# First pair's hash as four 32x32 diagonal tiles on TensorE, with the opening steps in another order

## Chip, cores and metric

The kernel runs on one core of one Trainium2 chip. The metric is the device time of one execution in microseconds (us). Matrix work runs on TensorE (PE, with PEld for its weight loads), elementwise work on VectorE (DVE), ScalarE (ACT) and GpSimd (POOL); SyncE (SP) only issues DMAs. Each engine has its own instruction queue and works through it in order.

## What is computed

The program is a bucketed attention followed by a gated feed-forward stage. For each of 4 batches and 8 heads, 768 tokens of 64 values are hashed: a token's six hash bits are the signs of its products with `proj`, and a query sees only the keys with the same six bits.

```python
q_bits = (np.einsum('bhsd,dk->bhsk', q, proj) > 0)
k_bits = (np.einsum('bhsd,dk->bhsk', k, proj) > 0)
mask = q_bucket[:, :, :, None] == k_bucket[:, :, None, :]      # bucket = the six bits as a number
scores = where(mask, scale * q @ k.T, -1e9)
x = softmax(scores) @ v                                        # then (3072, 512), heads side by side
g = x @ w_gate
out = x + sigmoid(x @ w_res) * ((gelu(g) * (x @ w_val)) @ w_out)
```

The hash is done in float32, since a sign must not flip; the rest of the matrix work is bfloat16.

## The kernel before

**Units.** Two heads of one batch are a pair; there are 16 pairs, four to a batch. A pair's q (or k) is a tile of 128 partitions x 12 columns x 64 values: column c 0 to 5 is the first head, 6 to 11 the second. In what follows, Q0-4 are columns 0 to 3 of the first pair's q, K2-6 columns 2 to 5 of its k, and so on, as the slices in the code have it. A pair's scores are made in nine chunks of 128x1024 (`scores`, L500); the step `('S', n)` is chunk n, S0 to S8 are the first pair, S9 to S17 the second. The exponential of a chunk is one ACT instruction (L511), and `('V', n)` multiplies it with the values (L475). The score chunks share two PSUM buffers (`sc_ps`).

**How bits come about for the first pair.** `tr` transposes q or k in 32x32 blocks on DVE (L273), so that 32 of the 64 values lie on each group of 32 partitions. `hash_one` (L318) multiplies with `projs`, a 128x128 matrix that carries `proj` four times on its diagonal in blocks of 32; a column's two halves (`dh`) add up in PSUM. `bits_one` (L323, L325) transposes the sums back on DVE and writes the signs as six extra values behind each token in `nat`, which already holds the token cast to bfloat16 by `cast` (L261 on ACT, L263 and L265 on POOL). `turn_pe` (L373) transposes `nat` on TensorE into PSUM, and `turned` (the step `copy`, L379 on ACT, L381 on DVE) copies it into `aug`, the operand of the scores. The other pairs of the first batch use `hash_mm` (L284), which hashes two or four operands at once with weights of 32 columns, each in a column strip of its own (`tile_position=(0, 32 * j)`).

**Order.** All tiles and semaphores come from the framework, but the order on every engine is the order in which the steps are written out in `PLAN`; nothing is rescheduled. `PLAN` covers the first batch's attention (S0 to S35); then come that batch's gate and value products (L525), and from there a loop puts a batch's feed-forward matmuls between the next batch's score chunks. SP issues the loads of q, k and v in the order of `PLAN`; a load into a buffer that is used again waits for the last reader of the old data. Each of `ld0` (q) and `ld1` (k) has four buffers, so the fifth load of a kind, `('load', 5, side)`, takes the first pair's buffer, and `('load', 4, side)` the second pair's.

**The opening.** `fill` issues matmuls of 70 columns on constants (L229), 4 + 44 + 4 of them, ahead of the first hash on TensorE. PSUM tags that matter: `av` has two buffers, `r` and `f` one each; `w0` and `w1` are the two score buffers, borrowed for two of the hashes. The framework orders accesses to one PSUM bank, so a turn into a bank waits for the copy that still reads it.

Of the kernel before, what the change touches and what calls it, by code (L numbers as in the profile page):

```python
# [9 lines left out]
FP32 = mybir.dt.float32  # L10
# [5 lines left out]

PLAN = [
    ('load', 1, 0), ('load', 1, 1), ('load_v', 0), ('load', 2, 0), ('load_v', 1), ('load', 2, 1),
    ('load', 3, 0), ('proj', 's', 'pssp'), ('proj', 'w', 'pppp'), ('cast', 0, 1, 'p', 0, 6),
# [10 lines left out]
    ('vs', 0), ('load', 4, 0), ('load', 5, 1), ('load', 4, 1), ('load_v', 3),  # L30
    ('S', 0),
    ('S', 1), ('hash1', 0, 1, 6, 12, 'av'), ('bits1', 0, 1, 6, 12), ('turn', 0, 0, 6, 12, 'av'),
    ('copy', 0, 0, 6, 12, 'v'),
    ('S', 2),
    ('S', 3), ('hash', (1,), 2), ('turn', 0, 1, 6, 12, 'f'), ('hash', (1,), 3), ('hash', (1,), 0),
# [57 lines left out]
def kernel(  # L93
# [12 lines left out]
    nc = tc.nc  # L106
    B, H, S, D = q.shape
    NBITS = proj.shape[1]
    DMODEL = H * D
    DFF = moe_w_gate.shape[1]  # L110
    P = 128
# [24 lines left out]
    const = ctx.enter_context(tc.tile_pool(name="const", bufs=1))  # L136
# [55 lines left out]
    nc.vector.memset(eps_sb, EPS)  # L192
    table = const.tile([P, 1], BF16, name="table")
    nc.scalar.activation(table, warm[:, 0:1], AF.Exp)
    projs = const.tile([P, 2, P], FP32, name="projs")
    nc.gpsimd.memset(projs, 0.0)
    projr = const.tile([P, NBITS, D], FP32, name="projr")
    projw = const.tile([P, 2, 32], FP32, name="projw")
    nc.gpsimd.memset(projw, 0.0)
# [16 lines left out]
    def spread(dst, engs):  # L216
        for a, eng in enumerate(engs):
            if eng is nc.scalar:
                nc.scalar.activation(dst(a), projn, AF.Copy)
            else:  # L220
                eng.tensor_copy(dst(a), projn)
# [30 lines left out]
    def nat_of(x):  # L252
        return nat[(2 * x[0] + x[1]) % NN]

    def cast(p, side, eng, c0=0, c1=HT):
        x = (p, side)
        scale = (1.0 / C) if side == 0 else 1.0
        sl = slice(c0, c1)
        dst = nat_of(x)[:, sl, 0:D]
        if eng is nc.scalar:  # L260
            nc.scalar.activation(dst, raw[x][:, sl], AF.Copy, scale=scale)  # L261
        elif side == 0:
            eng.tensor_scalar(dst, raw[x][:, sl], scale, 1.0, op0=ALU.mult, op1=ALU.mult)  # L263
        else:
            eng.tensor_copy(dst, raw[x][:, sl])  # L265

    t32, hsum, htok = {}, {}, {}
# [8 lines left out]
    def hash_mm(jobs, dhs=(0, 1), hs_=(0, 1)):  # L276
        if jobs[0] not in hsum:
            hsum[jobs[0]] = mm_ps.tile([P, HT, 32], FP32, tag="r", name="hs")
        hs = hsum[jobs[0]]
        for hh in hs_:  # L280
            sl = slice(hh * T, hh * T + T)
            for dh in dhs:
                for j, x in enumerate(jobs):
                    nc.tensor.matmul(hs[32 * j:32 * j + 32, sl], projw[:, dh, :],  # L284
                                     t32[x][:, sl, dh, :], start=(dh == 0), stop=(dh == 1),
                                     tile_position=(0, 32 * j))
# [24 lines left out]
    def hash_one(p, side, c0, c1, tag):  # L311
        n, x = c1 - c0, (p, side, c0)
        if tag in ("w0", "w1"):
            hsum[x] = (wpt, wps)[int(tag[1])][:, 0:2 * n * 32].rearrange("p (i c n) -> p i c n", i=2, c=n)
        else:
            hsum[x] = (av_ps if tag == "av" else mm_ps).tile([P, 2, n, 32], FP32, tag=tag, name="hs1")
        for dh in range(2):
            nc.tensor.matmul(hsum[x][:, 0], projs[:, dh, :], t32[p, side][:, c0:c1, dh, :],  # L318
                             start=(dh == 0), stop=(dh == 1))

    def bits_one(p, side, c0, c1):
        hs = hsum[p, side, c0]
# [37 lines left out]
        nc.sync.dma_start_transpose(out=ag, in_=nat_of(x).rearrange("p c n -> p (c n)"))  # L360
        aug[x] = ag

    pts = {}

    def turn_pe(p, side, c0, c1, tag, pool=mm_ps):
        x = (p, side)
        if x not in aug:
            aug[x] = aug_pool.tile([P, HT, P], BF16, tag=f"aug{side}", name=f"aug{side}")
        k = (p, side, c0 // T)
        if k not in pts:  # L370
            pts[k] = pool.tile([P, T, P], BF16, tag=tag, name="pt")
        for c in range(c0, c1):
            nc.tensor.transpose(pts[k][0:KA, c % T, :], nat_of(x)[:, c, 0:KA], ident)  # L373

    def turned(p, side, c0, c1, eng):
        dst = aug[p, side][0:KA, c0:c1, :]
        pt = pts[p, side, c0 // T][0:KA, c0 % T:c0 % T + c1 - c0]
        if eng is nc.scalar:
            nc.scalar.activation(dst, pt, AF.Copy)  # L379
        else:  # L380
            eng.tensor_copy(dst, pt)  # L381
# [27 lines left out]
    av = {}  # L409
# [46 lines left out]
    def x_turn(b, hp):  # L456
        pt = mm_ps.tile([P, T, P], BF16, tag="f" if b == 0 else "r", name="pt")
        for t in range(T):
            nc.tensor.transpose(pt[:, t, :], x_tok[b][:, hp, t, :], ident)  # L459
        if hp == HP - 1:  # L460
            nc.scalar.activation(x_sb[b][:, hp, 0:2], pt[:, 0:2], AF.Copy)
            nc.vector.tensor_copy(x_sb[b][:, hp, 2:T], pt[:, 2:T])
        else:
            nc.vector.tensor_copy(x_sb[b][:, hp], pt)
# [238 lines left out]
    def first_gv(i):  # L703
# [2 lines left out]
    STEP = dict(  # L706
        S=score, V=value, fill=fill, tr=tr,
        proj=lambda w, engs: spread(
            (lambda a: projs[32 * a:32 * a + 32, :, 32 * a:32 * a + NBITS]) if w == "s" else
            (lambda a: projw[32 * a:32 * a + 32, :, NBITS * a:NBITS * (a + 1)]),  # L710
            [ENG[e] for e in engs]),
        cast=lambda p, side, e, *c: cast(p, side, ENG[e], *c),
        hash1=hash_one,
        bits1=bits_one,
        turn=lambda p, side, c0, c1, tag: turn_pe(p, side, c0, c1, tag, POOLS[tag]),
        copy=lambda p, side, c0, c1, e: turned(p, side, c0, c1, ENG[e]),
        turn_dma=turn,
        hash=lambda ps, i: hash_mm([(p, side) for p in ps for side in range(2)], (i % 2,), (i // 2,)),
        tokens=tokens, bits=lambda p, side, e: bits(p, side, [ENG[x] for x in e]),
        va=vals_a, vs=vals_s, finish=finish, open=opened, preset=preset, repeat=repeat,  # L720
        w=load_w, load=load, load_v=load_v, xturn=lambda hp: x_turn(0, hp),
# [10 lines left out]
    for s in range(NSLOT, LAST):  # L732
        p, c = divmod(s, NCH)
# [60 lines left out]
```

## Time and profile before

| what | value |
|---|---|
| time, three runs | 338.42, 338.57, 338.58 us; median 338.57 us |
| profiled execution: span from the first to the last instruction | 337.2 us |
| profiled execution: own time apart from the span | none is given on its page |
| PE busy | 332.7 us (99%), 3086 matmuls |
| DVE, ACT, POOL busy | 216.4, 213.8, 175.0 us |
| mean DMA rate over the span | 130 GB/s |

The span is what the engines' instructions cover; the timed runs hold 1.4 us more than it. Times inside the trace are counted from the span's start. PE's busy share is no measure of slack, since matmuls are pipelined and a fill counts as busy; the chain of waits, which goes back from the last instruction to what released it, shows which engine sets the time in which stage.

### The profile page before, as it was taken

How to read it: one execution, taken by the hardware profiler on the slowest of the kernel's cores; microseconds unless marked ns; L12 is line 12 of the kernel's file. 1: busy time of each engine (PE TensorE's matmuls, PEld its weight loads, DVE VectorE, ACT ScalarE, POOL GpSimd, SP SyncE). 2: the span in 40 equal slices, each digit the busy share in tenths (PEclk: the TensorE clock that was granted, in tenths of full speed). 3: DMA queues.
4: the chain of work that ended last, by engine and by line, in shares of the span. 5: the costliest groups of instructions: out<-in, count | busy, mean ns of one | idle time of the engine just before them, and what ended most of it. 6: DMA issues, size and time to landing. Idle time of an engine off the chain costs nothing.

```text
span 337.2 us, 7740 instructions
## 1 busy us (share of the span) xinstructions
PE 332.7 (99%) x3086; PEld 205.2 (61%) x3086; DVE 216.4 (64%) x458; ACT 213.8 (63%) x247; POOL 175.0 (52%) x260
## 2 busy tenths in 40 slices
PE   8999999999999999999999999999999999999996
PEld 8677666565666655665666665666566665666444
DVE  7977675664577958875687896876567444343243
ACT  4889962237999962437999982255999984322220
POOL 4779930234489942575999982567978100000000
PEclk9999999999999999999999999999999999999999
DMA  7998999999966233516149933923140340000012
GB/s 218 372 297 127 207 246 196 188 150 194 319 225 169 61 97 80 106 37 126 63 110 275 268 109 91 137 47 65 32 126 33 80 101 33 31 2 0 31 64 94
DMA packets 74387, 43.88 MB, mean 130 GB/s; under 512 B 52544, under 2 KB 71360, under 8 KB 74352
## 3 DMA queue, kind: packets, MB, share of 16 engines
q1 hardware_dynamic: 67872, 37.95, 45.6%
q0 software_dynamic: 6400, 5.44, 10.4%
q8 instruction: 24, 0.39, 0.5%
q14 instruction: 11, 0.09, 0.1%
q10 hardware_dynamic: 80, 0.00, 0.0%
HBM read 29.56 MB, written 6.29 MB: 106 GB/s over the span
## 4 chain that ended last, share of the span: by engine, by line
PE 93%; ACT 3%; DVE 1%; POOL 1%; issue 1%; DVEq 0%; ACTq 0%
PE sp L525 37%; PE fps L571 18%; PE sp L500 16%; PE av L475 9%; PE rps L557 6%; PE hs L284 3%; ACT ering L511 3%; PE wps L229 1%; PE hs L318 1%; POOL pr L335 1%; PE pt L373 1%; ACT e L511 1%; DVE sums L341 1%; PE pt L459 0%; DVE o L577 0%
## 5 line engine op out<-in xcount | busy, mean ns | idle before, releaser
L511 ACT ACTIVATE e<-sp 128x1024 bf16<-128x1024 f32 x117 | 117.7, 1028 | 8.5 <-PE sp L500 3.4
L335 POOL TENSOR_TENSOR pr<-ld,projr 128x384 f32<-128x384 f32 x96 | 93.9, 998 | 46.3 <-DVE sums L341 27.7
L542 ACT ACTIVATE gt<-sp 128x768 bf16<-128x768 f32 x48 | 38.9, 811 | 83.5 <-PE sp L525 77.9
L500 PE MATMUL sp<-aug,aug 71*128 71x256 bf16 (+1 forms) x384 | 86.0, 325 | 0.3
L571 PE MATMUL fps<-wo,hh 128*128 128x512 bf16 (+2 forms) x312 | 79.6, 362 | 0.0
L545 DVE TENSOR_TENSOR hh<-gt,sp 128x768 bf16<-128x768 bf16 x48 | 45.8, 954 | 44.1 <-PE sp L525 40.8
L525 PE MATMUL sp<-x_sb,wg 128*128 128x512 bf16 (+1 forms) x384 | 70.9, 326 | 0.0
L525 PE MATMUL sp<-x_sb,wv 128*128 128x512 bf16 (+1 forms) x384 | 70.9, 326 | 0.0
L475 PEld LDWEIGHTS <-e 128*128 128x128 bf16 x936 | 43.5, 97 | 25.9
L341 DVE TENSOR_REDUCE sums<-pr 128x6 f32<-128x384 f32 x96 | 50.0, 541 | 11.5 <-POOL pr L335 11.0
L525 PEld LDWEIGHTS <-wg 128*128 128x128 bf16 x384 | 37.1, 98 | 25.6 <-issue 1.2
L525 PEld LDWEIGHTS <-wv 128*128 128x128 bf16 x384 | 37.5, 98 | 24.9 <-issue 0.2
L475 PE MATMUL av<-va,e 128*128 128x65 bf16 x936 | 47.0, 193 | 0.0
L571 PEld LDWEIGHTS <-hh 128*128 128x128 bf16 x312 | 28.1, 97 | 22.0 <-issue 0.2
L500 PEld LDWEIGHTS <-aug 71*128 71x128 bf16 x384 | 29.2, 97 | 11.1 <-issue 2.0
L574 DVE SCALAR_TENSOR_TENSOR fps<-th,fps 128x512 f32<-128x512 f32 (+2 forms) x26 | 17.0, 653 | 26.2 <-PE fps L571 26.0
L557 PE MATMUL rps<-wr,x_sb 128*128 128x512 bf16 x96 | 27.1, 379 | 0.0
L511 ACT ACTIVATE ering<-sp 128x1024 bf16<-128x1024 f32 x27 | 25.8, 1031 | 1.7 <-PE sp L500 1.4
L561 ACT ACTIVATE th<-rps 128x512 f32<-128x512 f32 x24 | 14.2, 594 | 18.5 <-PE rps L557 18.5
L273 DVE STREAM_TRANSPOSE t<-ld 128x768 f32<-128x768 f32 (+3 forms) x28 | 23.1, 844 | 0.7 <-PE hs L284 0.6
L454 DVE COPY av<-av 128x390 f32<-128x390 f32 x24 | 13.5, 563 | 11.9 <-PE av L450 11.7
L263 POOL TENSOR_SCALAR nat<-ld 128x768 bf16<-128x768 f32 (+1 forms) x12 | 9.6, 805 | 20.0 <-DMA aug<-nat 17.4
(76 smaller groups left out, 259.7 us busy)
## 6 DMA issues: line engine op xcount, KB each, us to landing
ldv<-in_v_dram SPq DMA_DIRECT2D x16, 384.0 KB, 5.6
out_dram<-o SPq DMA_DIRECT2D x23, 256.0 KB, 2.4
ld<-in_q_dram SPq DMA_DIRECT2D x15, 384.0 KB, 5.7
ld<-in_k_dram SPq DMA_DIRECT2D x15, 384.0 KB, 6.0
wg<-in_moe_w_gate_dram POOLq DMA_DIRECT2D x4, 384.0 KB, 9.1
wv<-in_moe_w_val_dram POOLq DMA_DIRECT2D x4, 384.0 KB, 10.2
wo<-in_moe_w_out_dram POOLq DMA_DIRECT2D x3, 512.0 KB, 7.5
wr<-in_moe_w_res_dram POOLq DMA_DIRECT2D x1, 512.0 KB, 15.7
```

Source lines behind the costliest of these rows:

```text
L273: nc.vector.transpose(t32[p, side][:, sl].rearrange("p c h n -> p (c h n)"), raw[p, side][:, sl].rearrange("p c d -> p (c d)"))
L335: nc.gpsimd.tensor_mul(pr, raw[x][:, hi * T:(hi + 1) * T], projr[:, bit].unsqueeze(1).to_broadcast([P, T, D]))
L341: nc.vector.reduce_sum(sums[x][:, hi * T:(hi + 1) * T, bit], pr, axis=mybir.AxisListType.X)
L475: nc.tensor.matmul(av[p, hi][:, qt, :], e[:, off:off + P], va[:, hi, jt, 0:D + 1], start=first, stop=(repeats(p, hi) and jt == T - 1), ski ...
L500: nc.tensor.matmul(sp[:, off:off + nq * P], ks[0:KA, hi * T + jt, :], qs[0:KA, hi * T + qt0:hi * T + qt0 + nq, :], start=True, stop=True)
L511: nc.scalar.activation(e, sp, AF.Exp, scale=float(ALPHA))
L525: nc.tensor.matmul(sp[:, c0:c1], w[:, kk, bass.ts(m, P)], xs[:, kk, c0:c1], start=(kk == 0), stop=(kk == KM - 1))
L542: nc.scalar.activation(gt, sp[:, 0:S], AF.Gelu)
L545: nc.vector.tensor_mul(hidden[b][:, m, :], gt, ps[1][:, 0:S])
L557: nc.tensor.matmul(rps, x_sb[b][:, kk, t, :], wr[:, kk, :], start=(kk == 0), stop=(kk == KM - 1))
L571: nc.tensor.matmul(fps[:, cs], hh[:, m, bass.ts(t, P)], wo[:, m, cs], start=(m == 0), stop=(m == KF - 1))
L574: nc.vector.scalar_tensor_tensor(fps[:, cs], th[:, cs], 1.0, fps[:, cs], op0=ALU.add, op1=ALU.mult)
```

## The change

The block-diagonal `projs` goes. A smaller `projc` holds `proj` once on each group of 32 partitions, in 32 columns of which six are used. `hash_one` issues four matmuls for each half instead of one: each takes the 32 partitions from `a` on, both as weights (32x32) and as data, writes the 32 PSUM partitions from `a` on, and stands at `tile_position=(a, a)`. `turn_pe` takes a new PSUM tile when the tag differs from the one that this operand's half had before.

In `PLAN`, up to S4: the 52 fills are one step; the first head's four hashes stand together, then its four `bits1`, then its turns, with Q4-6 turned into `av` instead of `r`; the cast of K6-12 goes from ACT to POOL; the two second-head transposes (`tr` of Q6-12 and K6-12) come after the first head's bits; the hash of Q6-12 stands behind S0 and that of K6-12 behind S1 (before: ahead of S0, and behind S1); the transposes of the second pair's operands (`tr`, 1, 0 and 1, 1) go from ahead of S0 to behind S1 and S2; the cast of the second pair's k goes ahead of `va`; all four hash steps of the second pair stand behind S3. From S4 on nothing is changed.

```diff
-    ('load', 3, 0), ('proj', 's', 'pssp'), ('proj', 'w', 'pppp'), ('cast', 0, 1, 'p', 0, 6),
-    ('cast', 0, 0, 'p', 6, 12), ('tr', 0, 0, 0, 4), ('cast', 0, 0, 's', 0, 6), ('fill', 4, 70),
-    ('cast', 0, 1, 's', 6, 12), ('tr', 0, 1, 0, 2), ('cast', 1, 0, 'p'), ('tr', 0, 0, 4, 6), ('fill', 44, 70),
-    ('fill', 4, 70), ('load_v', 2), ('tr', 0, 1, 2, 6), ('hash1', 0, 0, 0, 4, 'av'),
-    ('hash1', 0, 1, 0, 2, 'av'), ('bits1', 0, 0, 0, 4), ('bits1', 0, 1, 0, 2),
-    ('hash1', 0, 1, 2, 6, 'w1'), ('tr', 0, 0, 6, 12), ('bits1', 0, 1, 2, 6),
-    ('turn', 0, 1, 0, 2, 'f'), ('copy', 0, 1, 0, 2, 's'), ('turn', 0, 0, 0, 4, 'r'), ('hash1', 0, 0, 4, 6, 'w0'), ('load', 3, 1),
-    ('bits1', 0, 0, 4, 6), ('va', 0), ('tr', 0, 1, 6, 12),
-    ('copy', 0, 0, 0, 4, 's'), ('cast', 1, 1, 'p'), ('hash1', 0, 0, 6, 12, 'av'),
-    ('turn', 0, 1, 2, 6, 'f'), ('turn', 0, 0, 4, 6, 'r'), ('copy', 0, 1, 2, 6, 'v'),
-    ('bits1', 0, 0, 6, 12), ('tr', 1, 0), ('copy', 0, 0, 4, 6, 's'), ('tr', 1, 1), ('load', 5, 0),
+    ('load', 3, 0), ('load_v', 2), ('load', 3, 1), ('proj', 's', 'pssp'), ('cast', 0, 1, 'p', 0, 6),
+    ('proj', 'w', 'pppp'), ('cast', 0, 0, 'p', 6, 12), ('cast', 0, 0, 's', 0, 6), ('cast', 0, 1, 'p', 6, 12),
+    ('tr', 0, 0, 0, 4), ('tr', 0, 1, 0, 2), ('tr', 0, 0, 4, 6), ('tr', 0, 1, 2, 6), ('fill', 52, 70),
+    ('hash1', 0, 0, 0, 4, 'av'), ('hash1', 0, 1, 0, 2, 'av'), ('hash1', 0, 0, 4, 6, 'w0'), ('hash1', 0, 1, 2, 6, 'w1'),
+    ('bits1', 0, 0, 0, 4), ('bits1', 0, 1, 0, 2), ('bits1', 0, 0, 4, 6), ('bits1', 0, 1, 2, 6),
+    ('turn', 0, 1, 0, 2, 'f'), ('copy', 0, 1, 0, 2, 's'), ('turn', 0, 0, 0, 4, 'r'), ('copy', 0, 0, 0, 4, 's'),
+    ('turn', 0, 0, 4, 6, 'av'), ('copy', 0, 0, 4, 6, 's'), ('turn', 0, 1, 2, 6, 'f'),
+    ('tr', 0, 0, 6, 12), ('copy', 0, 1, 2, 6, 'v'), ('tr', 0, 1, 6, 12),
+    ('cast', 1, 0, 'p'), ('cast', 1, 1, 'p'), ('va', 0), ('load', 5, 0),
+    ('S', 0), ('hash1', 0, 0, 6, 12, 'av'), ('bits1', 0, 0, 6, 12),
     ('vs', 0), ('load', 4, 0), ('load', 5, 1), ('load', 4, 1), ('load_v', 3),
-    ('S', 0),
-    ('S', 1), ('hash1', 0, 1, 6, 12, 'av'), ('bits1', 0, 1, 6, 12), ('turn', 0, 0, 6, 12, 'av'),
+    ('S', 1), ('hash1', 0, 1, 6, 12, 'av'), ('tr', 1, 0), ('bits1', 0, 1, 6, 12), ('turn', 0, 0, 6, 12, 'r'),
     ('copy', 0, 0, 6, 12, 'v'),
-    ('S', 2),
-    ('S', 3), ('hash', (1,), 2), ('turn', 0, 1, 6, 12, 'f'), ('hash', (1,), 3), ('hash', (1,), 0),
-    ('copy', 0, 1, 6, 8, 's'), ('tr', 2, 0), ('hash', (1,), 1),
+    ('S', 2), ('turn', 0, 1, 6, 12, 'f'), ('copy', 0, 1, 6, 8, 's'), ('tr', 1, 1),
+    ('S', 3), ('hash', (1,), 2), ('hash', (1,), 3), ('hash', (1,), 0), ('hash', (1,), 1), ('tr', 2, 0),
...
-    projs = const.tile([P, 2, P], FP32, name="projs")
-    nc.gpsimd.memset(projs, 0.0)
+    projc = const.tile([P, 2, 32], FP32, name="projc")
+    nc.gpsimd.memset(projc[:, :, NBITS:32], 0.0)
...
         for dh in range(2):
-            nc.tensor.matmul(hsum[x][:, 0], projs[:, dh, :], t32[p, side][:, c0:c1, dh, :],
-                             start=(dh == 0), stop=(dh == 1))
+            for a in range(0, P, 32):
+                nc.tensor.matmul(hsum[x][a:a + 32, 0], projc[a:a + 32, dh, :], t32[p, side][a:a + 32, c0:c1, dh, :],
+                                 start=(dh == 0), stop=(dh == 1), tile_position=(a, a))
...
-        if k not in pts:
+        if pt_tag.get(k) != tag:
+            pt_tag[k] = tag
             pts[k] = pool.tile([P, T, P], BF16, tag=tag, name="pt")
...
-            (lambda a: projs[32 * a:32 * a + 32, :, 32 * a:32 * a + NBITS]) if w == "s" else
+            (lambda a: projc[32 * a:32 * a + 32, :, 0:NBITS]) if w == "s" else
```

More of the change, by code (lines that the diff above doesn't have):

```diff
@@ L361, in turn @@
         aug[x] = ag
-    pts = {}
+    pts, pt_tag = {}, {}
     def turn_pe(p, side, c0, c1, tag, pool=mm_ps):
```

## Prediction, on record before the result

> **What bounds the kernel now.** I read the page first, for the shares, then the chain of waits from the start, then the order of time engine by engine up to S4, where the two plans meet again.
>
> ```profile
> span 337.2 us, 7740 instructions
> ...
> PE 93%; ACT 3%; DVE 1%; POOL 1%; issue 1%; DVEq 0%; ACTq 0%
> ```
>
> The chain of waits (start, length, what; a piece ends when its result is there):
>
> ```profile
> 0.84 3.19 PE wps L229 x52
> 4.04 1.81 PE hs L318 x8
> 5.85 0.94 PE wps L318 x4
> 6.79 0.34 PE pt L373 x6
> 7.12 0.45 PE wpt L318 x4
> 7.57 0.71 PE hs L318 x4
> 8.28 0.42 PE pt L373 x6
> 8.69 0.43 PE sp L500 x2
> ...
> 9.75 0.65 PE hs L318 x4
> 10.40 0.34 PE pt L373 x6
> 10.74 1.00 PE sp L500 x5
> 11.74 0.45 PE hs L284 x4
> 12.19 0.46 PE pt L373 x6
> 12.65 1.10 PE hs L284 x12
> 13.75 0.54 PE sp L500 x3
> 14.29 0.49 PE av L475 x16
> ...
> 21.68 1.44 PE hs L284 x32
> ```
>
> The reader is to see that from 0.84 on hardly a piece is anything but TensorE. It goes without a pause from the fills through four first-head hashes, the turns and S0 to S4, whose result is there at 13.75 + 0.54 = 14.29. So whatever S4 loses or gains is lost or gained, provided nothing behind it gives way. Later ACT takes over:
>
> ```profile
> 23.70:34.20 10.50, 10.26 (x158) 7.54 (x155) 8.19 (x24) 10.41 (x12) 9.37 (x19) 1.00 0.77 137
> ```
>
> In that window ACT is busy for 10.41 of 10.50 us (the fourth busy column): there is no slack to take up a delay, and afterwards the chain is TensorE again. I therefore carry a shift of S4 one to one to the end.
>
> **The tiles themselves.** A float32 matmul is two records, so a hash of two halves is four passes. Warm, four passes of 192 columns take 0.65: 0.163 each, 0.85 ns a column. Warm, four of 64 columns (wpt) take 0.45, 0.11 each, where the columns alone need 0.054: the load of 128 weight columns binds. That load also shows the clock (duration min/median/max, first and last start):
>
> ```profile
> L318 PEld LDWEIGHTS wps<-t,projs x4: 333/333/333, 5.5 to 6.2; 128*128 128x128 f32 x4
> L318 PEld LDWEIGHTS wpt<-t,projs x4: 190/192/192, 6.9 to 7.2; 128*128 128x128 f32 x4
> ```
>
> The same load falls from 333 to 192 ns between 6.2 and 6.9, so I take TensorE at half speed until then: 0.217 a pass for 128 columns, 0.108 for 64. The x8 piece, 1.81 for a 128-column and a 64-column hash, fits: 0.22 a pass for both, the short one bound by its weights. With 32 weight columns that bound goes, if the four tiles run abreast. No diagonal tile is in the trace; the nearest row is L284, weights of 32 columns in four strips. 32 records in 1.44 are eight rounds of 0.163 (1.30) and 0.14 for entering: four abreast, into the same bank. I take that. So K0-2 falls from four passes of 0.22 to four of 0.108, minus 0.45; Q4-6 moves into the slow stretch and costs 0.43 there, about the 0.45 it cost before; hashes of 128 and 192 columns gain nothing, since their columns bind. A hash now has 16 matmuls. They could be bound by issue: by the 16 of L475 in 0.49, K0-2 and Q4-6 cost 0.06 more each; by L284's 0.045 a record, 0.29 more each. I take none of it, since L284's time is its columns', and keep 0.6 for the range.
>
> Changing between whole array and strips costs: two rounds of L284 take 0.45 where 0.325 is due, the six turns behind them 0.46 where 0.34 is usual. That is 0.12 a change. Before there are four such changes up to S4; after there are eight (into and out of the first four hashes, of Q6-12, of K6-12, and of the second pair's hash): plus 0.48. So TensorE's own work is about even, and the order decides.
>
> **The order.** The rows of DVE and ACT before:
>
> ```profile
> 6.28 0.57 DVE L273 STREAM_TRANSPOSE t<-ld 128x384 f32<-128x384 f32 x1
> 6.83 0.33 DVE L323 STREAM_TRANSPOSE wps<-wps 128x128 f32<-128x128 f32 x1
> 7.19 0.18 DVE L325 TENSOR_SCALAR nat<-wps 128x24 bf16<-128x24 f32 x1
> 8.61 0.42 DVE L381 COPY aug<-pt 71x512 bf16<-71x512 bf16 x1
> 8.95 0.38 DVE L323 STREAM_TRANSPOSE hs<-hs 128x192 f32<-128x192 f32 x1
> 9.37 0.20 DVE L325 TENSOR_SCALAR nat<-hs 128x36 bf16<-128x36 f32 x1
> 9.48 1.83 DVE L273 STREAM_TRANSPOSE t<-ld 128x768 f32<-128x768 f32 x2
> 11.73 0.54 DVE L381 COPY aug<-pt 71x768 bf16<-71x768 bf16 x1
> ```
>
> ```profile
> 7.09 0.52 ACT L261 ACTIVATE nat<-ld 128x384 bf16<-128x384 f32 x1 [2.91 <-DMA ld<-in_k_dram]
> 7.52 0.85 ACT L379 ACTIVATE aug<-pt 71x256 bf16<-71x256 bf16 x2
> 8.73 0.38 ACT L379 ACTIVATE aug<-pt 71x256 bf16<-71x256 bf16 x1 [0.36 <-PE pt L373]
> 9.16 3.99 ACT L511 ACTIVATE ering<-sp 128x1024 bf16<-128x1024 f32 x4
> ```
>
> *First head.* The fills end at 4.04 as before (52 in the same place of TensorE's queue). Then 0.12 for the change and 0.87 + 0.43 + 0.43 + 0.87 for the four hashes: 6.76, where before K2-6 ended at 6.79. Another 0.12 and six turns of 0.056: Q0-4 is turned at 7.22, K0-2 at 6.99. ACT no longer stands behind the cast that waited for the k load (7.09, after 2.91 idle): it copies both in 0.85, from 7.03 to 7.88, before until 8.37. S0 restarts TensorE from a wait, which adds 0.17 of filling (S0 and S1 run 1.23 from start to end, below, against 1.06 on the chain): 7.93 + 0.43 + 0.17 = 8.53. The first exponential starts at 8.57 instead of 9.16. So far the change gains 0.6.
>
> ```profile
> 8.53 1.23 PE L500 MATMUL sp<-aug,aug 71*128 71x512 bf16 x5
> ```
>
> *Second head.* Now TensorE has the hash of Q6-12 still to do, which before was done by 8.28: 8.53 + 0.12 + 0.65 = 9.30. S1: 0.12 + 0.43, 9.85. K6-12: 10.62. Turn Q6-12 (0.12 + 0.34): 11.08. S2: 11.51. DVE meanwhile: bits of K2-6 6.80 to 7.34; `tr` of Q6-12 (0.57), which before lay in DVE's wait for that hash, now stands behind it, to 7.85; the copy of K2-6 waits for its turn, 7.95 to 8.37; `tr` of K6-12 to 8.87; idle; bits of Q6-12 (0.62) 9.34 to 9.96; `tr` 1,0 (half of 1.83) to 10.80; bits of K6-12 to 11.34; copy of Q6-12 to 11.80; `tr` 1,1 to 12.64 (neighbours overlap by 0.08). Before, the two second-pair transposes were done at 11.31, ahead of the bits of K6-12.
>
> TensorE turns K6-12 behind those bits, until 11.90, and S3 is done at 12.33. Now the wait that the change adds: the second pair's hash needs `tr` 1,1, so its k half starts at 12.69, where TensorE alone would be there at 12.45. Behind it in TensorE's queue stands S4, and ACT waits for S4. Eight rounds of 0.163 and 0.17 of filling: 14.16; S4 (0.54): 14.70, against 14.29. **Plus 0.41.** Without that wait S4 would end at 14.29, no gain: the head start of 0.6 has gone into four changes of mode and three waits of TensorE.
>
> *The rest of the move costs nothing that shows.* POOL gets the cast of K6-12 (0.5) at 7.09, when the k half lands, and stands idle from there to its cast of the second pair (8.19, after 2.29 idle); were that cover gone, the turn of K6-12, some 4 us later, would still hide it. The second pair's k cast goes ahead of `va`, into another wait of POOL.
>
> ```profile
> 8.19 0.83 POOL L263 TENSOR_SCALAR nat<-ld 128x768 bf16<-128x768 f32 x1 [2.29 <-DMA ld<-in_q_dram]
> 11.34 1.44 SPq L161 DMA_DIRECT2D ld<-in_k_dram x2
> ```
>
> On SP the loads up to `load` 3,1 keep their order. `load` 4,0 and 4,1 take the buffers that `tr` 1,0 and 1,1 read, and so wait until 10.8 and 12.7; before, 4,1 was the second of the two k issues that ended at 12.78. What stands behind it, one load of v, is for the fourth pair. The plan reads these data only behind S20.
>
> The sum stands against the profiled 337.2: 337.6. The median of the runs lies 1.37 above that span, which I leave as it is: 338.57 + 0.41, **339.0 us**. About 0.2%, 0.68 us, is what a measurement of this kernel can tell from no change, so this forecast is "same, on its slow side". By its own bounds (issue +0.6, DVE's chain 0.2 either way) it reaches from 338.6 to 339.7.
>
> **Rivals.**
>
> *The array stays slow for longer.* The half speed ended near 6.6, after 5.7 us of fills and whole-array hashes. Four diagonal tiles use a quarter of one pass's cells. If they don't count as work, the fast stretch begins only after the turns and scores have run for a while; it decides if loads are still at 333 ns behind 7 us. Doubled until S1 are the turns (0.34), S0 (0.43) and the hash of Q6-12 (0.65), +1.4: 340.4. Against it: there are as many passes as before. The Trainium skill's "TensorE: Matmul & The Clock Gate", Part 1, says that a free-running window of some 3.4 us of PE activity opens the gate; the trace can't show what a quarter-full array counts for. By that rule a missed window moves the step to about 10 us, which is near this price.
>
> *The tiles don't run abreast.* Then the change doesn't do what it says: each of the four first-head hashes takes four times its time. At half speed until 6.6 and full speed after, their end moves from 6.76 to about 10.5 (+3.8), and each second-head hash adds 1.95: about 346. Against it stands L284, four strips into one bank. The Trainium skill's "TensorEngine Tiling (Array Packing)", Restrictions and Gotchas, says that different row tiles cannot access the same PSUM bank at once, and here all four write one; L284's strips are column tiles, so no run here shows the rule or breaks it, and by it the time is this rival's.
>
> *The waits don't come.* If DVE runs ahead and TensorE never waits, its work alone gives 6.76 + 0.79 (turns) + 0.43 + 0.77 + 0.55 + 0.77 + 0.46 + 0.43 + 0.34 + 0.43 + 1.42 + 0.54 = 13.69 for S4, minus 0.6: 338.0. That needs K2-6's bits, which can't begin before 6.80, ahead of the turns; somewhere between this and 338.5 is possible, beyond it only if changes of mode are cheaper for these tiles.
>
> **How the numbers follow.** Forecast 0.58 (0.42 within 0.2%, 0.16 above, from the issue bound); slow array 0.16, slower; tiles one after another 0.10, slower; no waits 0.16 (0.09 faster, 0.07 within). So faster 0.09, same 0.49, slower 0.42. The range goes from 338.1, within the third rival, to 340.6, just over the first; outside are the 346 and half of the third.
>
> **What would show it.** Right: the first ACT exponential near 8.6, L318's 64-column hash in about 0.43, TensorE idle before L284 until `tr` 1,1 ends near 12.6, the first V behind S4 at 14.7 instead of 14.29, and everything behind it shifted alike. Wrong: loads or turns at half speed after 7 us (first rival), records of L318 one behind another (second), no idle before L284 (third), or a shift at S4 that the 23.7 to 34.2 stretch doesn't show.

## The result: 1.40 us slower, paid at the two ends of the kernel

| kernel | median of its runs | lowest to highest | runs |
|---|---|---|---|
| before | 338.78 us | 338.34 to 340.50 | 20 |
| changed | 340.18 us | 339.12 to 341.02 | 20 |

The ratio is 1.0039, 95% interval 1.0031 to 1.0047: slower by 1.40 us (1.05 to 1.59), above the 0.2% that the prediction took for what can be told from no change. Of all the experiments below, one run was slow (346.53 us, of `e12`), and its ratio leaves that run out.

The profiled execution of the changed kernel took 340.53 us, about 2.05 more than its span. Between 2.0 and 2.1 lie between time and span in every run of it, and in those of the kernel before, so the 337.2 of the kernel before belongs to an execution of about 339.3, in the upper part of its runs. The 1.37 us that the prediction put outside the span are thus about 2.05 outside the span, less some 0.7 by which the profiled execution was slower than the median.

From the page of the changed kernel, and below it one line of the page of before:

```profile
span 338.5 us, 7838 instructions
...
q8 instruction: 25, 0.41, 0.5%
```

```profile
q8 instruction: 24, 0.39, 0.5%
```

New are 72 weight loads and the 72 matmuls that go with them (the page counts only 98 instructions more than before's 7740, since some matmul records are missing), and one packet more on q8, the queue that brings instructions: 25 packets in 0.41 MB are 16.4 KB each. That packet will matter.

The opening, from the chain of waits of the changed kernel (start, length, what):

```profile
4.07 1.50 PE hs L316 x32
5.57 0.29 PE wpt L316 x16
5.87 0.44 PE wps L316 x16
6.30 0.26 PE pt L372 x2
6.56 0.02 issue
6.58 0.87 ACT aug L378 x2
7.46 0.04 issue
7.50 0.59 PE sp L499 x2
8.09 0.78 PE hs L316 x16
8.87 0.54 PE sp L499 x3
9.41 0.78 PE hs L316 x16
10.20 0.46 PE pt L372 x6
10.65 0.44 PE sp L499 x3
11.09 0.02 issue
11.11 0.50 PE pt L372 x6
11.61 0.43 PE sp L499 x2
12.04 1.81 PE hs L281 x16
13.85 0.54 PE sp L499 x3
```

Its waits in the first 20 us have the line that the prediction asked for, TensorE's second-pair hash waiting for `tr`:

```profile
PEld hs L281 <- DVE t L270: 0.3, 1, 0.3
```

The exponentials in the order of time, ACT of the changed kernel and then one row of before:

```profile
8.13 1.02 ACT L510 ACTIVATE ering<-sp 128x1024 bf16<-128x1024 f32 x1 [0.41 <-PE sp L499]
...
14.43 1.95 ACT L510 ACTIVATE ering<-sp 128x1024 bf16<-128x1024 f32 x2 [1.10 <-PE sp L499]
```

```profile
14.33 1.95 ACT L511 ACTIVATE ering<-sp 128x1024 bf16<-128x1024 f32 x2 [0.91 <-PE sp L500]
```

S0 is exponentiated at 8.13 instead of 9.16, S4 at 14.43 instead of 14.33: a head start of 1.03 us becomes a lag of 0.10. This lag stays the same up to about 200 us and is 0.18 from 204 on. Then comes the end, from the order of time: the last `th` (the sigmoid's ACT instruction), SP's issues of the last four outputs and DVE's last instruction, changed and before:

```profile
331.60 0.60 ACT L560 ACTIVATE th<-rps 128x512 f32<-128x512 f32 x1 [2.86 <-PE rps L556]
...
332.25 3.72 SPq L578 DMA_DIRECT2D out_dram<-o  x4
...
334.63 0.29 DVE L576 SCALAR_TENSOR_TENSOR o<-fps,x_tok 128x128 f32<-128x128 f32 x1
```

```profile
331.42 0.60 ACT L561 ACTIVATE th<-rps 128x512 f32<-128x512 f32 x1 [2.86 <-PE rps L557]
...
332.07 3.03 SPq L579 DMA_DIRECT2D out_dram<-o  x4
...
334.45 0.29 DVE L577 SCALAR_TENSOR_TENSOR o<-fps,x_tok 128x128 f32<-128x128 f32 x1
```

The last computed value is there 0.18 later than before, but the span ends 1.2 later: 3.53 us after that value where before it was 2.50. SP begins its four issues 0.18 late and needs 3.72 us for them, not 3.03. The DMA view of the last 8 us, changed and before, shows what else was there:

```profile
q8 instruction: 1, 0.02, 1.0%
...
out_dram<-o SPq DMA_DIRECT2D x1, 256.0 KB, 4.3
out_dram<-o SPq DMA_DIRECT2D x1, 128.0 KB, 3.0
out_dram<-o SPq DMA_DIRECT2D x2, 64.0 KB, 2.2
```

```profile
out_dram<-o SPq DMA_DIRECT2D x1, 256.0 KB, 2.0
out_dram<-o SPq DMA_DIRECT2D x1, 128.0 KB, 1.7
out_dram<-o SPq DMA_DIRECT2D x2, 64.0 KB, 1.5
```

The last column is the time from issue to landing. In the changed kernel all four outputs land later, and a q8 packet lies among them; before has no q8 packet there. In the trace's DMA records it starts at 333.77 and takes 1.35 us. TensorE has 6201 records before and 6346 in a second profile of the changed kernel (`e6`); in the first one 47 are missing. From one such packet to the next, TensorE starts 251 of them on average. So 145 more, 144 of the tiles and one wait, move every packet and bring the 25th close to TensorE's end: ten records are left behind its start in this profile, 28 in `e6`. Before, the last one starts at 322.79 with 153 records left, where no output is waited for. The Trainium skill's "Runtime: NRT & Kernel Launch", Instruction fetch mechanics, says that instructions come in 16 KiB blocks of 256, and that crossing a block's edge is mostly hidden. The size agrees with this trace, and the number nearly does. In this profile the block at the end does not look hidden: the outputs that travel beside it land late.

So the theory to test was: **most of the loss is the block at the end (by the count of instructions, whatever they do), and a few tenths are the opening.** Its rivals: the tiles themselves cost it, or the order.

### The profile page after: what moved, and what is told of

It is laid out like the page before. It is cut to its first block, busy times and chain, and to the rows that moved or that the text cites. A ratio compares the mean times of both kernels' runs of the same rounds, so it can differ in the third digit from the quotient of the medians.

```text
span 338.5 us, 7838 instructions
## 1 busy us (share of the span) xinstructions
PE 330.1 (98%) x3111; PEld 203.5 (60%) x3158; DVE 216.0 (64%) x458; ACT 213.4 (63%) x246; POOL 175.5 (52%) x261
## 4 chain that ended last, share of the span: by engine, by line
PE 92%; ACT 4%; DVE 1%; issue 1%; POOL 1%; DVEq 0%; ACTq 0%
PE sp L524 37%; PE fps L570 17%; PE sp L499 16%; PE av L474 9%; PE rps L556 6%; PE hs L281 3%; ACT ering L510 3%; PE wps L226 1%; PE hs L316 1%; POOL pr L333 1%; ACT e L510 1%; PE pt L372 1%; DVE sums L339 1%; PE pt L458 0%; DVE o L576 0%
## 5 line engine op out<-in xcount | busy, mean ns | idle before, releaser
L570 PE MATMUL fps<-wo,hh 128*128 128x512 bf16 (+2 forms) x287 | 74.4, 361 | 1.3
L556 PE MATMUL rps<-wr,x_sb 128*128 128x512 bf16 x91 | 26.0, 379 | 0.2
```

The costliest lines, as they stand in the source:

```text
L556: nc.tensor.matmul(rps, x_sb[b][:, kk, t, :], wr[:, kk, :], start=(kk == 0), stop=(kk == KM - 1))
L570: nc.tensor.matmul(fps[:, cs], hh[:, m, bass.ts(t, P)], wo[:, m, cs], start=(m == 0), stop=(m == KF - 1))
```

## Experiments

Every time stands beside runs of the kernel before on the same chip.

### One half of the change at a time

The diagonal tiles with the plan of before (`e1_tiles_alone`), and the new plan with the 128x128 weights (`e2_order_alone`).

```diff
 e1:  PLAN as before; hash_one, projc and turn_pe as changed
 e2:  PLAN as changed; hash_one and projs as before
```

> The plan of before with the diagonal tiles: the tiles alone. Theory A (instruction block): TensorE's instructions are fetched in blocks of 16384 bytes, about one per 256 instructions; the tiles add 144, so that one more block comes while the last outputs are sent. Then the last block starts about 0.5 us before TensorE's end, an output's DMA issue takes about 1 us instead of 0.33, and the time is 0.8 to 1.2 us above before. Theory B (opening): the loss comes from the new order and its changes of mode, and the end of that one profile was chance; then the tiles alone give before within 0.3 us.

> The plan of after with the 128x128 block-diagonal weights: the order alone, with no instruction more on TensorE than before. Theory A: no block at the end, only what the opening costs, 0.2 to 0.7 us above before. Theory B: the whole 1.4 us or more, since the order carries the loss.

Before had 339.12. Tiles alone: 339.60, ratio 1.0024 (1.0012 to 1.0035), less than the 0.8 to 1.2 us that were expected. Order alone: 339.88, ratio 1.0039 (1.0020 to 1.0057), a little above the 0.2 to 0.7 us of theory A and well below the 1.4 of theory B. Tiles alone keep the 144 instructions, and have a block in the last 8 us (`q8 instruction: 1, 0.02, 1.2%` there); from the start of the last `th` to the end they take 6.16 us, before 5.82. Order alone has no such block and a normal end of 5.81; its profiled execution loses in the opening, where S4 is exponentiated at 14.88.

Five of order alone's twelve runs lie apart from the others, at 341.35 to 341.72 against 339.10 to 340.17. The median of the other seven, 339.25, is only 0.13 above before, and the profiled execution (340.17) is the slowest of them. A single profiled run of the same program fell into the upper group too:

> The order alone again, for a second profile: its runs fell into two groups, 339.1 to 340.2 and 341.4 to 341.7. If this one falls into the upper group, its trace shows where 2 us go: theory A expects one long wait on a DMA beside an instruction block, theory B expects it in the opening, ahead of S5. In the lower group: as the first profile, S4 0.3 to 0.6 us behind before.

It took 341.42 us. The weight loads of the first-head hashes, by form: above this run (`e10_order_again`), below `e2_order_alone`:

```profile
L315 PEld LDWEIGHTS wps<-t,projs x4: 333/333/333, 6.4 to 7.1; 128*128 128x128 f32 x4
```

```profile
L315 PEld LDWEIGHTS wps<-t,projs x4: 192/192/192, 6.3 to 6.7; 128*128 128x128 f32 x4
```

At 7.1 us this load still takes 333 ns. The clock record has the rise to full speed at 9.77 us, against 6.02 in `e2_order_alone`, and S4's exponential comes at 16.13 instead of 14.88. This is the first rival's mechanism, at a price of 1.25 us between the two profiled runs (the prediction had 1.4), but in a kernel without any diagonal tile. Between the two groups of timed runs lie 2.4 us; the timed runs have no record of when the clock rose, so how far this explains them is open.

### The number of instructions, and nothing else

`e3`: the changed kernel with 26 fills of 140 columns, so 52 instructions fewer at the same fill time. `e4`: the kernel before with 124 fills of 29 columns, 144 instructions more, as many as the tiles bring.

```diff
 e3   -('fill', 52, 70)
      +('fill', 26, 140)
 e4   -('fill', 4, 70) ... ('fill', 44, 70) ... ('fill', 4, 70)
      +('fill', 4, 29) ... ('fill', 116, 29) ... ('fill', 4, 29)
```

> The changed kernel with 26 fills of 140 columns instead of 52 of 70: the same TensorE time in the opening, 52 instructions less. Theory A: the last block is not reached any more, the end is as in before, and about 1 us of the loss is gone: 0.2 to 0.6 us above before. Theory B: as the changed kernel, 1.4 us above before.

> The kernel before with 124 fills of 29 columns instead of 52 of 70: 144 TensorE instructions more and nothing else; the fills may end up to 0.3 us later. Theory A: 0.8 to 1.3 us above before, with a block in the last microsecond of TensorE. Theory B: before within 0.3 us.

`e4`: 340.19 us against 339.12, ratio 1.0034 (1.0023 to 1.0046). Not a line of the hash or of the order differs from before, and most of the loss is there. Its first hash matmul starts 0.24 later, at 4.15, since the fills take longer; the rest has to come from somewhere else, and its end has the block again, from 332.94 on for 1.33 us. SP's issues, from its order of time:

```profile
331.82 3.29 SPq L579 DMA_DIRECT2D out_dram<-o  x4
```

From the last `th` to the end: 6.28, 0.46 more than before. The 0.24 and the 0.46 make 0.70 of the 1.07 us. The profiled execution (339.49) is the fastest of six, and where the others lose the rest is not shown.

`e3` was expected to win and lost: 340.56, ratio 1.0050 (1.0038 to 1.0063). Its end is normal (5.81), as the theory says. But the block before that has moved as well, from 262.4 to 266.2, and there TensorE now waits for a transposing DMA. Waits from 265 to 269 us, and the DMA view from 255 to 272:

```profile
PEld L499 <- DMA aug<-nat: 1.3, 1, 1.3
```

```profile
aug<-nat SPq DMA_TRANSPOSE x1, 5.5
```

In the changed kernel the same transpose lands after 3.7 us. Between two neighbouring exponentials there the lag grows by 1.36 us. So the expectation failed: the loss did not shrink, it grew. The theory was widened: a block can cost time wherever a DMA on which TensorE depends is under way, not at the end alone.

### A count that puts all blocks back

107 fills of 34 columns make 255 instructions more than before, one block, so every block behind the opening should lie nearly where it lay before. On the changed kernel (`e5`), with the changed kernel itself beside it (`e6`), and on tiles alone (`e7`).

```diff
 e5   -('fill', 52, 70)
      +('fill', 107, 34)
 e7   tiles alone, fills 4 + 99 + 4 of 34 columns
```

> The changed kernel with 107 fills of 34 columns (3.0 us together, as 52 of 70): 110 TensorE instructions more, so with the tiles' 145 nearly one whole block of 256 more than before. Theory A, as it stands after the first four runs (an instruction block that lands on the last outputs, or on a transposing DMA that a score waits for, costs about 1 us; where the blocks land is set by the number of instructions ahead): all blocks behind the opening lie where they lay before, the last one near 322, and only the opening's cost is left, 0.1 to 0.5 us above before. Theory B (the opening and its order carry the loss): 1.2 us or more above before, as the changed kernel.

> The changed kernel itself, for the same chip as the others of this call, and a second profile. Theory A: 1 to 1.5 us above before, a block in TensorE's last microsecond, and at least one DMA near it held up. Theory B: the same time, but an end like that of before.

> The tiles alone (the plan of before) with 107 fills of 34 columns, blocks as before. Theory A: the end's loss of the tiles alone is gone and their gain in the opening is left: 0 to 0.4 us below before. Theory B: as the tiles alone, 0.8 us above before.

Before had 339.00. `e5`: 339.25, ratio 1.0006 (0.9998 to 1.0015), no longer to be told from no change. `e6`: 339.69, ratio 1.0024 (1.0013 to 1.0035). SP's last four issues in `e5`, from its order of time:

```profile
332.03 3.03 SPq L578 DMA_DIRECT2D out_dram<-o  x4
```

`e5` has 110 instructions *more* than `e6` and is 0.44 us faster: its last block starts at 322.73, no q8 packet is in its last 6 us, and its end takes 5.80, as in before. In `e6` a block of 1.50 us starts at 333.48, the same four issues take 3.37, and the end 6.54. Here the changed kernel loses 0.69, though, not 1.40; the 1 to 1.5 us that were expected of it did not come.

`e7` missed: 339.40, ratio 1.0025 (1.0005 to 1.0044), not to be told from tiles alone, although its end is normal (5.79). Two of its twelve runs lie apart at 342.2, like those of order alone; without them the median is 339.33. In its profile ACT's cast of K6-12, which in this plan stands ahead of the copies, waits for the load of k until 7.30 (7.09 in before):

```profile
7.30 0.52 ACT L261 ACTIVATE nat<-ld 128x384 bf16<-128x384 f32 x1 [3.02 <-DMA ld<-in_k_dram]
```

The chain of waits goes through this load, and S4's exponential comes at 14.65, a lag of 0.32. Another 0.2 us come in near 41 us, where ACT idles for 0.21. Why it pauses there, and what the runs of tiles alone lose without the block at the end, is open.

### Another bad place for a block

40 fills of 91 columns, 24 instructions fewer than the changed kernel.

```diff
 e9   -('fill', 52, 70)
      +('fill', 40, 91)
```

> The changed kernel with 40 fills of 91 columns (3.0 us together): 24 TensorE instructions less, so that the last block should just not be reached, while all others start only some 24 instructions later. Theory A (a block in the last microsecond holds up the last outputs): the stretch from the last tanh to the end is 5.8 us as in every profile without such a block, instead of 6.2 to 6.9, and the time is 0.3 to 0.8 us below the changed kernel's (339.7 to 340.2), unless a block now meets a transposing DMA, which would show as a stall of TensorE on aug of about 1 us. Theory B: the end stays long.

340.80 against 338.76, ratio 1.0062 (1.0050 to 1.0074): the largest loss of all by the ratio, with a normal end (5.80). The case that the expectation set apart came about, at another transpose first. From 203 to 207 us TensorE waits for the transpose of the feed-forward's input (waits; then the DMA view from 198 to 208):

```profile
PE sp L524 <- DMA x_sb<-x_tok: 1.1, 1, 1.1
```

```profile
q1 hardware_dynamic: 1014, 0.60, 39.8%
...
x_sb<-x_tok SPq DMA_TRANSPOSE x1, 4.0
```

The changed kernel has in the same window 999 packets on q1 with 19.8% of the engines' time, and the transpose lands after 2.8 us. Here hardly more packets take twice the time, beside a block that starts at 203.68. The lag grows by 1.21 us at this place, and by 0.39 at 267, where the next block meets the `aug` transpose.

### The opening

`e11`: the kernel before with only the cast of K6-12 moved from ACT to POOL. `e12`: `e5` without the new wait (`tr` 1,1 ahead of DVE's copy, Q6-12 turned into `av`). `e8`: `e5` with V0 and V1 ahead of the second pair's hash, so that ACT gets S4 later but TensorE has work while it waits for `tr` 1,1.

```diff
 e11  -('cast', 0, 1, 's', 6, 12)
      +('cast', 0, 1, 'p', 6, 12)
 e12  -('turn', 0, 0, 6, 12, 'r'), ('copy', 0, 0, 6, 12, 'v') ... ('copy', 0, 1, 6, 8, 's'), ('tr', 1, 1)
      +('turn', 0, 0, 6, 12, 'av'), ('tr', 1, 1), ('copy', 0, 0, 6, 12, 'v') ... ('copy', 0, 1, 6, 8, 's')
 e8   -('S', 3), ('hash', (1,), 2)
      +('S', 3), ('V', 0), ('V', 1), ('hash', (1,), 2)
```

> The kernel before with one step of the change: the cast of K6-12 on POOL instead of ACT. The number of instructions on TensorE stays, so all blocks lie as before. ACT no longer waits for the k load ahead of its copies. If S0 is bound by TensorE's own work there, as the chain of before says, it gains 0 to 0.1 us; if by ACT's wait where the load comes late, 0.2 to 0.4 us.

> The changed kernel with 107 fills of 34 columns, where the transpose of the second pair's k stands ahead of the copy of Q6-12 on DVE, and Q6-12 is turned into av, so that the second pair's hash waits for neither. If that wait is what the opening costs, S4 comes 0.3 to 0.4 us earlier than in the changed kernel with 107 fills (exponential of S4 near 13.9 to 14.0 instead of 14.3), and the time falls by as much, to before or 0.2 us below it. If not, it stays at 0.2 to 0.3 us above before.

> The changed kernel with 107 fills of 34 columns, and with V0 and V1 ahead of the second pair's hash instead of behind S4, so that TensorE has work while it waits for the transpose of the second pair's k. If that wait of about 0.4 us is what the opening costs, S5 comes 0.4 us earlier than in the changed kernel with 107 fills, and the time is 0.3 to 0.5 us below that one's. If something else sets S4 and S5 (ACT, or the copy of K6-8), it is the same within 0.1 us.

`e11`: 338.99 against 338.76, ratio 1.0003 (0.9990 to 1.0017). No difference is seen, but the interval goes from -0.34 to +0.58 us, so neither of the two gains that were named is ruled out.

`e12`: 339.24 against 338.76, ratio 1.0013 (1.0004 to 1.0022). The wait is gone, as the chain shows; above the second pair's hash of `e5`, below that of `e12`:

```profile
11.90 1.81 PE hs L281 x16
```

```profile
12.38 1.42 PE hs L281 x16
```

0.39 us of wait are gone from TensorE's chain; the median does not show them (`e5`, beside other runs of before, had 1.0006). S4's exponential comes at 14.38 against 14.29 in `e5`, but the clock rose at 6.43 here and at 4.81 there. What the wait is worth once this is allowed for stands in the next section.

`e8`: 339.48 against 339.00, ratio 1.0012 (1.0000 to 1.0025), a miss. Its chain has a wait of its own:

```profile
3.68 7.82 DMA ldv<-in_v_dram
11.50 0.05 issue
11.55 0.83 POOL va L385
```

V0 needs `va`, and POOL can only make it when the load of v lands at 11.50. The wait for `tr` was replaced by the wait for v, and S4's exponential came at 15.17.

None of these versions beats the kernel before.

## Why the prediction was right, and where it was not

The measured 340.18 lies in the range (338.1 to 340.6), on the side that had a chance of 0.42. It does not lie within the forecast's own bounds (338.6 to 339.7; the terms named for them, 0.6 above and 0.2 either way, would give 338.8 to 339.8). That the range holds it is luck: its upper end was set by the slow array, which did not happen here.

**The tiles run abreast: right.** K6-12's hash, 16 matmuls, takes 0.78 us: 0.65 as before and 0.13 for the change of mode (predicted 0.12). In `e1`, where Q6-12's hash follows another hash of tiles, it takes 0.65. The second rival, tiles one after another at about 346, is refuted. The Trainium skill's "TensorEngine Tiling (Array Packing)", Gotcha 1, by which row tiles cannot access one PSUM bank at the same time, does not hold for these four, which write different partitions of one bank: if the four had to take turns, the hash would take about four times 0.65. The bound from issue, up to 0.29 a hash, did not come: the first two hashes take 1.50 where 1.42 was worked out.

**S0 earlier: right, and by more.** The first-head hashes end at 6.31, predicted 6.76, and S0's exponential comes at 8.13, predicted 8.57. The clock rose at 5.59 in this execution and at 6.63 in before's. The prediction took the time of the rise in one execution for a property of the kernel. In thirteen of the fourteen profiles it lies between 3.8 and 6.6 us, and in one at 9.8.

**The head start is lost: right.** S0 led by 1.03, and S4 lags by 0.10. The places are the predicted ones, the two hashes behind S0 and S1 and the wait for `tr` 1,1: from the end of S3 to the second pair's last hash column 1.81 us, predicted 1.83 (12.33 to 14.16). What was predicted too late at 6.76, by 0.45, is still 0.31 too late at S4.

**Plus 0.41 for the opening: in accord with the profiles, once the clock is allowed for.** When the clock rises differs from one execution to the next, and S4 moves with it. Start of S4's exponential by the time of the rise, in the profiled executions (without `e8`, where V0 and V1 stand ahead, and `e10`):

| opening | executions: rise, S4's exponential (us) |
|---|---|
| before's | `before` 6.63, 14.33; `e11` 3.92, 13.36; `e4` (fills 0.24 longer) 5.25, 14.08 |
| changed | `e9` 4.61, 14.21; `e5` 4.81, 14.29; `e3` 4.81, 14.31; changed 5.59, 14.43; `e6` 6.03, 14.63 |
| changed, no wait for `tr` 1,1 | `e12` 6.43, 14.38 |
| tiles with the plan of before | `e1` 5.32, 13.90; `e7` 5.07, 14.65 |
| new plan with 128x128 weights | `e2` 6.02, 14.88 |

The five changed openings, which differ in their fills alone, lie within 0.06 of a line of 0.26 us for each us that the rise comes later. Carried on to the rise of `before`, 6.63, this line gives 14.76, where `before` has 14.33: 0.43 later, predicted 0.41. `e12` lies 0.32 ahead of the line and 0.05 behind `before`, predicted 0.0 ("Without that wait S4 would end at 14.29"). So the lag of 0.10 in the profile is a cost of about 0.4 us, less what an earlier rise gave back, and the wait is most of it. In `e2` and `e6` the clock rose at the same time, and they differ in the tiles alone: with the tiles S4 comes 0.25 earlier, so the tiles are not what the opening costs.

This rests on few executions: the line is carried 0.6 us past its last point, to one execution of before. The executions with the plan of before can't give a line of their own, since there something else moves S4 too. In `e1`, `e4`, `before` and `e7` ACT's cast behind the load of k starts at 6.17, 6.68, 7.09 and 7.30, and S4's exponential comes in the same order, at 13.90, 14.08, 14.33 and 14.65; the times of the rise have another order. In `e11` that cast is not on ACT, its first copies start at 6.05, and S4's exponential comes earliest of all, at 13.36. The runs agree less well: `e5` loses 0.25 us, with an interval of -0.07 to +0.51, and `e12` 0.44 (0.14 to 0.75), where by the line it should lose less. That the wait is what the opening costs is thus shown in the profiles only.

**The step that failed** is "I therefore carry a shift of S4 one to one to the end", with "*The rest of the move costs nothing that shows*". The shift was carried to 331 us (0.10 to 0.18), and there 1.03 us more came in, with the packet on q8. The prediction counted the tiles' extra matmuls, but only as time to issue them: it gave that 0.6 us in the range and nothing in the sum. That 145 more instructions move every instruction block, and bring one to the place where the last outputs are issued, was not a term at all. The row was on the page of before (24 packets on q8). Over the four profiles with a block at the end (`e1`, `e4`, `e6` and the changed kernel), last `th` to end takes 6.16, 6.28, 6.54 and 6.86 us; without one, in ten, 5.79 to 5.83. A half clock at the end is no rival: in all four the clock falls to half within the last 1.8 us of the span, but it does so in `e2` as well (at 337.12 of 337.98), whose end is normal. The missing term is thus 0.34 to 1.04 us, 0.65 in the mean. With it, the sum would have been 338.57 + 0.41 + 0.65 = 339.63.

**The slow array** at 340.4 is the rival nearest in time, and is not what happened: weight loads and turns ran at full speed behind 6 us. It did happen in the order alone.

**Still open.** Opening about 0.43 (by the line) and end 0.65 make 1.08; the runs gave 1.40 (1.05 to 1.59) in the first series, which holds it near its lower end, and 0.69 (0.44 to 1.19) beside `e5`, which holds it near its upper end. Why the two series differ is not known. How a 16 KB packet makes SP's issues longer (3.72 instead of 3.03) and doubles the time of other packets was not tried. Nor is it known why order alone missed its clock window in what may be five of twelve runs, where the 0.08 us near 204 in the changed kernel come from, and why the medians do not show what `e12` gains in its profile.

## What to carry to other kernels

When a change adds instructions to an engine that runs to the end, work out where its instruction blocks will lie afterwards, and what DMA is being waited for there; `e5` and `e9`, which differ only in the number of fills that make up the same fill time, stand at 1.0006 and 1.0062. Before a loss of a few tenths of a per cent is put down to the edit, run the edit with the count brought back by fills of equal total length. That is no full guard, as `e7` shows, which kept its loss. And compare single profiles of an opening only with the time of the clock's rise, and of the loads that it waits for, beside them.

## What the runs showed of the hardware

- An instruction block (16.4 KB, 0.9 to 1.8 us on its queue in the fourteen profiles) passes unnoticed almost everywhere: of the 25 in the changed kernel, one stands beside a loss of about 1 us, and between S4 and the last `th` the lag grows by 0.08 us in all. Where it met a transposing DMA that TensorE waited for, the transpose took 4.0 instead of 2.8 us and 5.5 instead of 3.7.
- Four tiles of 32x32 on the diagonal take the time of one pass of the whole array, 0.163 us for 192 columns of float32 at full speed, into one PSUM bank.
- In thirteen of fourteen executions of much the same opening the array came to full speed between 3.8 and 6.6 us, and in one at 9.77. In every profile the first stretch at full speed lasts 331.09 or 334.51 us, which are 97 and 98 times 3.413 us: the clock changes by steps of such a window. The Trainium skill's "TensorE: Matmul & The Clock Gate", Part 1, states a free-running window of some 3.4 us, and these stretches agree with it. One window ahead of 9.77 is 6.36, within the span of the others, so one window was missed there, and that execution took 1.25 us longer than the other one profiled of the same program.
